# Five loads instead of seven, pieces of 53 and 11 rows, and the final wait on another engine

## The chip, the cores and the metric

The kernel runs on one core of a Trainium2 chip. The metric is device time in microseconds (us) of one execution; "the span" in a profile is shorter, from the first to the last instruction of the kernel's own program. A "landing" is the last of the 16 semaphore updates that report a transfer as complete. A change counts as faster or slower from 2% on. All times below are medians of several executions (granted clock 1.00 in every profile).

## The reference

```python
B, S, D = 1024, 16, 512            # bf16
def reference(x, y, gamma):        # x, y: (B, S, D); gamma: (D)
    return x + gamma * y
```

x and y have 16.78 MB each, the output too: 50.33 MB must cross between HBM and SBUF. One multiply and one add per element are all the arithmetic.

## The kernel before

The 16,384 rows of 512 elements are laid out as 128 partitions of 128 rows; "rows" below counts within a partition. y stays in SBUF whole and the result is written over it. x has a smaller buffer, part of which is used twice. SP issues the loads, ScalarE (ACT) issues the load of gamma and the two stores of 64 rows each, VectorE (DVE) multiplies and adds in four pieces, and TensorE (PE) spreads gamma over the partitions by a matmul with ones and then passes on a release: the stores may start when the load `RELEASE` has landed.

```python
PIECES = [40, 37, 40, 11]
# x entries: first row, end row, place in the x buffer; y entries: first row, end row
SP = [('x', 0, 40, 0), ('y', 0, 40), ('x', 40, 77, 40), ('y', 40, 77),
      ('y', 77, 128), ('x', 77, 117, 0), ('x', 117, 128, 40)]
ACT = [('g',), ('s', 0, 64), ('s', 64, 128)]
EARLY = (2, 1)                     # that many issues of SP and ACT go ahead of the first barrier
RELEASE = ('x', 77, 117, 0)
DVE = [('m', 0), ('a', 0), ('m', 1), ('a', 1), ('m', 2), ('a', 2), ('m', 3), ('a', 3)]
...
def frees(w):                      # which adds must be done before load w may overwrite x rows
    old = x_loads[: x_loads.index(w)]
    old = [v for v in old if meets(v[3], v[3] + v[2] - v[1], w[3], w[3] + w[2] - w[1])]
    return [c for v in old for c in pieces_of(v[1], v[2])]
...
_take(s_load[RELEASE], 16, nc.tensor)      # TensorE: that load has landed
nc.tensor.sem_inc(s_go, 1)                 # ACT may issue the stores
nc.tensor.sem_inc(s_rel, 1)                # DVE may read it
...
nc.scalar.sem_inc(s_end, 1)                # the end of the program
_take(s_end, 1, nc.sync)
_take(s_add, n, nc.sync)
_take(s_out, 16 * len(stores), nc.sync)    # SP waits until the stores have landed
```

`_take(sem, n, eng)` lets an engine wait until a semaphore has n and takes n off it.

Of the kernel before, what the change touches and what calls it, by code (L numbers as in the profile page):

```python
# [3 lines left out]


PIECES = [40, 37, 40, 11]



SP = [('x', 0, 40, 0), ('y', 0, 40), ('x', 40, 77, 40), ('y', 40, 77), ('y', 77, 128), ('x', 77, 117, 0), ('x', 117, 128, 40)]  # L10
ACT = [('g',), ('s', 0, 64), ('s', 64, 128)]

EARLY = (2, 1)


RELEASE = ('x', 77, 117, 0)

DVE = [('m', 0), ('a', 0), ('m', 1), ('a', 1), ('m', 2), ('a', 2), ('m', 3), ('a', 3)]
MULT, ADD = mybir.AluOpType.mult, mybir.AluOpType.add


def _take(sem, n, eng):


    return eng.wait_ge(sem, n).then_inc(sem, -n)  # L25


def kernel(
# [9 lines left out]
    nc = tc.nc  # L38
# [8 lines left out]
    rows = N // P  # L47
    n = len(PIECES)
    assert sum(PIECES) == rows
    starts = [sum(PIECES[:c]) for c in range(n + 1)]  # L50
    dt = xf.dtype
# [7 lines left out]
    y_sb = nc.alloc_sbuf_tensor("y_sb", [P, rows, D], dt).ap()  # L59
    x_loads = [w for w in SP + ACT if w[0] == "x"]  # L60
    y_loads = [w for w in SP + ACT if w[0] == "y"]
    stores = [w for w in SP + ACT if w[0] == "s"]
    for loads in (x_loads, y_loads, stores):
# [8 lines left out]
    s_add, s_go, s_rel, s_end, s_out = sem("s_add"), sem("s_go"), sem("s_rel"), sem("s_end"), sem("s_out")  # L72
    added = [a for kind, *a in DVE if kind == "a"]
    order = {a[0]: k for k, a in enumerate(added)}

    def meets(a, b, c, d):
        return a < d and c < b

    def pieces_of(a, b):
        return [c for c in range(n) if meets(starts[c], starts[c + 1], a, b)]  # L80

    def x_at(row):
        return next(w[3] + row - w[1] for w in x_loads if w[1] <= row < w[2])

    def frees(w):

        old = x_loads[: x_loads.index(w)]
        old = [v for v in old if meets(v[3], v[3] + v[2] - v[1], w[3], w[3] + w[2] - w[1])]
        return [c for v in old for c in pieces_of(v[1], v[2])]

    early = []

    def ring(eng, what, n_early):

        known, went = 0, False
        for k, w in enumerate(what):
            kind = w[0]
            need = frees(w) if kind == "x" else pieces_of(w[1], w[2]) + list(w[3:]) if kind == "s" else []
            need = max((order[c] + 1 for c in need), default=0)
            if kind == "s" and not went:  # L100
                _take(s_go, 1, eng)
                went = True
            if need > known:
                eng.wait_ge(s_add, need)
                known = need
            if kind == "g":
                i = eng.dma_start(out=gamma_row, in_=gamma.unsqueeze(0)).then_inc(s_gamma, 16)
            elif kind == "x":
                to = x_sb[:, w[3] : w[3] + w[2] - w[1], :]
                i = eng.dma_start(out=to, in_=xv[:, w[1] : w[2], :]).then_inc(s_load[w], 16)  # L110
            elif kind == "y":
                r = slice(w[1], w[2])
                i = eng.dma_start(out=y_sb[:, r, :], in_=yv[:, r, :]).then_inc(s_load[w], 16)
            else:
                r = slice(w[1], w[2])
                i = eng.dma_start(out=ov[:, r, :], in_=y_sb[:, r, :]).then_inc(s_out, 16)
            if k < n_early:
                early.append(i.ins)

    ring(nc.sync, SP, EARLY[0])  # L120
    ring(nc.scalar, ACT, EARLY[1])
# [9 lines left out]

    _take(s_load[RELEASE], 16, nc.tensor)
    nc.tensor.sem_inc(s_go, 1)
# [4 lines left out]
    def need(loads, c):  # L138
        for w in loads:
            if w not in landed and meets(starts[c], starts[c + 1], w[1], w[2]):  # L140
                if w == RELEASE:
                    _take(s_rel, 1, nc.vector)
                else:
                    _take(s_load[w], 16, nc.vector)
                landed.add(w)

    for kind, *args in DVE:
        c = args[0]
        yt = y_sb[:, starts[c] : starts[c + 1], :]
        if kind == "m":  # L150
            need(y_loads, c)
            g = gamma_sb[:, None, :].to_broadcast([P, PIECES[c], D])
            nc.vector.tensor_tensor(out=yt, in0=yt, in1=g, op=MULT).then_inc(s_dve, 1)  # L153
            open_mults += 1
        else:
# [4 lines left out]
            at = x_at(starts[c])  # L160
            xt = x_sb[:, at : at + PIECES[c], :]
            nc.vector.tensor_tensor(out=yt, in0=xt, in1=yt, op=ADD).then_inc(s_add, 1)  # L162


    nc.scalar.sem_inc(s_end, 1)
    _take(s_end, 1, nc.sync)
    _take(s_add, n, nc.sync)
    _take(s_out, 16 * len(stores), nc.sync)

    main = nc.main_func.blocks[0].instructions  # L170
    names = {i.name for i in early}
# [35 lines left out]
```

## Time and profile before

| | before |
|---|---|
| time | 119.99 us (119.98 to 120.29) |
| profiled execution | 120.14 us, span 118.8 us |
| VectorE busy | 70.2 us, 59% |
| the 16 DMA engines' busy share, both queues | 66.0 + 32.6 = 98.6% |
| last add ends / second store issued | 97.44 / 97.47 us |
| last packet ends / last landing seen | 118.45 / 118.78 us |

The first thing to read is the DMA share: it leaves no room. Two kinds of record are used besides the page: that of each DMA packet (start, duration, size, queue), and that of semaphore updates, which goes on after the span's end. The packet record does not name the DMA engine; where one engine is followed below, the end of a packet was matched with the start of the next. The runtime closes every execution with a barrier over the five engines, a reset of semaphores and another barrier, and the reported time includes this: the last barrier update of the profiled execution comes at 120.258 us after the span's start, beside a reported 120.14.

### The profile page before, as it was taken

Reading aid. Unit: us, or ns where it says so; the run is one execution under the profiler, and the core shown is the slowest. Engines: PE = TensorE matmul, PEld = TensorE weight load, DVE = VectorE, ACT = ScalarE, POOL = GpSimd, SP = SyncE. Lnnn points to the kernel's source line nnn. Section 1 sums busy time; section 2 is a strip of 40 time slices with the busy share of each in tenths; the row PEclk is TensorE's granted clock in tenths of the full one; section 3 lists DMA queues with packets and bytes.
Section 4 is the critical chain, followed back from the end, with each engine's and each line's share of the span. In section 5 each row is a group of like instructions: output and inputs, shape, how many; then the busy total and the mean of one; then the engine's idle time right before and its main releaser. Section 6 shows DMA issues by size and latency. Waiting matters only on the chain. (4 is left out here: it accounts for less than half of the span.)

```text
span 118.8 us, 84 instructions
## 1 busy us (share of the span) xinstructions
PE 0.6 (0%) x1; PEld 0.1 (0%) x1; DVE 70.2 (59%) x10; POOL 0.2 (0%) x4
## 2 busy tenths in 40 slices
PE   0100000000000000000000000000000000000000
PEld 0000000000000000000000000000000000000000
DVE  0020000009999999799999999999999980000000
POOL 0000000000000000000000000000000000000000
DMA  7999999999999999989696999998899889988890
GB/s 221 442 441 441 441 441 441 441 425 408 408 421 472 485 459 408 475 369 563 281 563 262 441 414 441 408 637 353 353 530 530 353 353 397 662 353 353 353 684 22
DMA packets 1298, 50.33 MB, mean 424 GB/s; under 512 B 145, under 2 KB 146, under 8 KB 146
## 3 DMA queue, kind: packets, MB, share of 16 engines
q1 hardware_dynamic: 1008, 33.55, 66.0%
q10 hardware_dynamic: 290, 16.78, 32.6%
HBM read 33.56 MB, written 16.78 MB: 424 GB/s over the span
## 5 line engine op out<-in xcount | busy, mean ns | idle before, releaser
L153 DVE TENSOR_TENSOR y_sb<-y_sb,gamma_sb 128x20480 bf16<-128x20480 bf16 (+2 forms) x4 | 34.8, 8688 | 20.6 <-DVEq L25 20.6
L162 DVE TENSOR_TENSOR y_sb<-x_sb,y_sb 128x20480 bf16<-128x20480 bf16 (+2 forms) x4 | 34.8, 8691 | 0.6
L129 DVE CAST gamma_sb<-gamma_ps 128x512 bf16<-128x512 f32 x1 | 0.7, 690 | 4.1 <-DVEq L25 4.1
L124 DVE MEMSET ones_row<- 1x128 bf16 x1 | 0.2, 165 | 2.0 <-PEq L41 2.0
L127 PE MATMUL gamma_ps<-gamma_row,ones_row 1*128 1x512 bf16 x1 | 0.6, 581 | 5.5 <-PEq L25 5.5
L127 PEld LDWEIGHTS gamma_ps<-gamma_row,ones_row 1*128 1x128 bf16 x1 | 0.1, 98 | 5.5 <-issue 5.5
L191 POOL MEMSET const-bfloat16-1.0<- 128x1 bf16 x1 | 0.1, 102 | 0.0
L191 POOL MEMSET const-uint8-127<- 128x1 uint8 x1 | 0.1, 101 | 0.0
L191 POOL MEMSET const-float32-0.0<- 128x1 f32 x1 | 0.1, 99 | 0.2 <-issue 0.2
L191 POOL MEMSET const-float32-1.0<- 128x1 f32 x1 | 0.1, 98 | 0.0
## 6 DMA issues: line engine op xcount, KB each, us to landing
x_sb<-in_x_dram SPq DMA_DIRECT2D x2, 5120.0 KB, 21.3
y_sb<-in_y_dram SPq DMA_DIRECT2D x1, 6528.0 KB, 61.8
y_sb<-in_y_dram SPq DMA_DIRECT2D x1, 5120.0 KB, 26.3
x_sb<-in_x_dram SPq DMA_DIRECT2D x1, 4736.0 KB, 36.0
y_sb<-in_y_dram SPq DMA_DIRECT2D x1, 4736.0 KB, 46.9
x_sb<-in_x_dram SPq DMA_DIRECT2D x1, 1408.0 KB, 10.6
out_dram<-y_sb ACTq DMA_DIRECT2D x2, 21.8
gamma_row<-in_gamma_dram ACTq DMA_DIRECT2D x1, 1.0 KB
```

The source lines that it names most:

```text
L124: nc.vector.memset(ones_row, 1.0).then_inc(s_ones, 1)
L127: nc.tensor.matmul(gamma_ps, ones_row, gamma_row, start=True, stop=True).then_inc(s_ps, 1)
L129: nc.vector.tensor_copy(out=gamma_sb, in_=gamma_ps).then_inc(s_dve, 1)
L153: nc.vector.tensor_tensor(out=yt, in0=yt, in1=g, op=MULT).then_inc(s_dve, 1)
L162: nc.vector.tensor_tensor(out=yt, in0=xt, in1=yt, op=ADD).then_inc(s_add, 1)
L191: nc = _bacc.Bacc("TRN2", target_bir_lowering=False, num_devices=1)
```

## The change

Its intent: fewer and larger transfers, a last add that ends earlier, and the final wait on another engine.

```diff
-PIECES = [40, 37, 40, 11]
+PIECES = [53, 11, 53, 11]
-SP = [('x', 0, 40, 0), ('y', 0, 40), ('x', 40, 77, 40), ('y', 40, 77), ('y', 77, 128), ('x', 77, 117, 0), ('x', 117, 128, 40)]
+SP = [('y', 0, 64), ('x', 0, 64, 0), ('y', 64, 128), ('x', 64, 117, 0), ('x', 117, 128, 64)]
-RELEASE = ('x', 77, 117, 0)
+RELEASE = ('x', 64, 117, 0)
-DVE = [('m', 0), ('a', 0), ('m', 1), ('a', 1), ('m', 2), ('a', 2), ('m', 3), ('a', 3)]
+DVE = [('m', 0), ('m', 1), ('a', 0), ('a', 1), ('m', 2), ('m', 3), ('a', 2), ('a', 3)]
 ... (frees() now counts only the pieces whose rows are really overwritten)
-    _take(s_end, 1, nc.sync)
-    _take(s_add, n, nc.sync)
-    _take(s_out, 16 * len(stores), nc.sync)
+    _take(s_end, 1, nc.tensor)
+    _take(s_add, n, nc.tensor)
+    _take(s_out, 16 * len(stores), nc.tensor)
```

The last x load (11 rows) gets rows of the buffer that nothing used before. The two stores stay as they were.

More of the change, by code (lines that the diff above doesn't have):

```diff
@@ L85, in frees @@
     def frees(w):
-        old = x_loads[: x_loads.index(w)]
-        old = [v for v in old if meets(v[3], v[3] + v[2] - v[1], w[3], w[3] + w[2] - w[1])]
-        return [c for v in old for c in pieces_of(v[1], v[2])]
+        c = set()
+        for v in x_loads[: x_loads.index(w)]:
+            lo, hi = max(v[3], w[3]), min(v[3] + v[2] - v[1], w[3] + w[2] - w[1])
+            if lo < hi:
+                c |= set(pieces_of(v[1] + lo - v[3], v[1] + hi - v[3]))
+        return sorted(c)
     early = []
```

## The prediction

> **What bounds the kernel now.** I read the page's slices and engine table first, then the timeline, then the record of each DMA packet, then the waits, and last what follows the span's end.
>
> ```profile
> span 118.8 us, 84 instructions
> PE 0.6 (0%) x1; PEld 0.1 (0%) x1; DVE 70.2 (59%) x10; POOL 0.2 (0%) x4
> DVE  0020000009999999799999999999999980000000
> DMA  7999999999999999989696999998899889988890
> q1 hardware_dynamic: 1008, 33.55, 66.0%
> q10 hardware_dynamic: 290, 16.78, 32.6%
> 1.00:98.50 97.50, 0.58 (x1) 0.10 (x1) 70.20 (x10) 0.00 (x0) 1.00 1.00 431
> ```
>
> The reader should see: VectorE is busy 59% of the span and idle in the last seven slices; the 16 DMA engines are busy 66.0 + 32.6 = 98.6% of it. The last line is one long window (columns: the stretch in us from the start, its length, engines' busy times, clock, DMA share, GB/s): from 1.00 to 98.50 us the DMA share is 1.00. The kernel moves 50.33 MB and its time is the DMA engines' time, plus a start and an end. The low digits 6 to 8 are an artefact of large packets counted in slices; the window shows no hole.
>
> ```profile
> 0.00 0.37 SPq L110 DMA_DIRECT2D x_sb<-in_x_dram  x1
> 26.84 10.83 DVE L153 TENSOR_TENSOR y_sb<-y_sb,gamma_sb 128x20480 bf16<-128x20480 bf16 x1 [19.94 <-DVEq L25]
> 48.67 21.18 SPq L110 DMA_DIRECT2D x_sb<-in_x_dram  x2
> 77.07 20.74 ACTq L116 DMA_DIRECT2D out_dram<-y_sb  x2
> 94.35 3.09 DVE L162 TENSOR_TENSOR y_sb<-x_sb,y_sb 128x5632 bf16<-128x5632 bf16 x1
> L162 DVE TENSOR_TENSOR y_sb<-x_sb,y_sb 128x20480 bf16<-128x20480 bf16 x2 | 21.6, 10824 | 0.3
> ```
>
> The last add ends at 94.35 + 3.09 = 97.44, and the second store is issued at 97.47 (the two issues are merged in the ACTq line: 77.07 + 20.74 is the end of the second). The first store's packets end between 98.47 and 98.93 on the 16 engines. A store becomes ready about 1.01 us after its issue: the very first load, issued at 0.00, has its first packet at 1.00. So the second store arrived just in time, with no slack. In the packet record twelve engines begin it within a few ns of the end of the first, but four begin some 24 to 139 ns late (ends and starts paired in order) and their first packet takes 2.45 to 2.46 us, not 2.418. The latest of them, starting at 99.06, is the engine that ends the program's traffic at 118.45; the next one ends at 118.25. So I read the late last add as costing about 118.45 - 118.25 = 0.20 us now. This is the only stall by computation that I find.
>
> **What the Trainium skill says.** "DMA: Bandwidth & Descriptors", section "Where 436 GB/s comes from", gives 16 ports x 32 B x 850 MHz, 435 GB/s in all, or 27.2 GB/s a port. The trace agrees: a 65,536-byte packet takes 2.418 us, 27.1 GB/s. The same page, "Issuing engines are not separate DMA queues": DMAs from different engines share the same 16 DMA engines, so splitting them otherwise buys no bandwidth; the 1.00 share, with loads on one queue and stores on the other, agrees. "VectorE: DVE Perf Modes", "The perf-mode tier table": a bf16 tensor_tensor stops at two elements a cycle; 20,480 / 2 / 0.96 GHz = 10.67 us, and the trace has 10.82. "Runtime: NRT & Kernel Launch", "The ~15µs preamble/postamble breakdown": after the kernel comes a barrier that passes serially over five engines at 44 ns a hop, then a reset of semaphores and another barrier. The trace's semaphore updates after the span agree on the hop: 98.080, 98.118, 98.161 us are 38 and 43 ns apart.
>
> **The change part by part.**
>
> Packets. Each transfer is 128 rows of one packet, 8 to an engine. Median packet times in the trace: 11,264 B 0.422 us, 37,888 B 1.401, 40,960 B 1.514, 52,224 B 1.928, 65,536 B 2.418. A line through the first and last gives 36.78 ns per KB (1,000 B) plus 8 ns per packet. The seven loads of before need 8 x (3 x 1.514 + 2 x 1.401 + 1.928 + 0.422) = 77.55 us of an engine. The five of after need 8 x (3 x 2.418 + 2.004 + 0.422) = 77.44, where 2.004 is the line's value for 53 rows, 54,272 B. Bytes are equal, so removing two loads removes only 16 packets' overhead: **-0.11 us**, all on the path.
>
> Order of loads. The big ones still follow each other in one queue. With the start as now (the slowest engine ended the first load at 14.25, 2.14 after 8 x 1.514) I get landings, noticed about 0.45 later, at: y 0-64 21.9, x 0-64 41.3, y 64-128 60.6, x 64-117 76.6, x 117-128 79.9.
>
> VectorE. Same elements, eight instructions as before; the 53-row one is 27,136 / 2 / 0.96 GHz + 0.16 = 14.29 us, the 11-row one 3.09. Two multiplies from 22.0 to 39.4; two adds wait for x, 41.3 to 58.8; two multiplies wait for y, 60.7 to 78.1; the adds 78.2 to 95.7. The idle start of VectorE shrinks and a new idle time of about two times 1.9 us appears, all hidden. x 64-117 overwrites rows 0-53 of x and waits for the add that ends at 55.7; it is then ready at 56.7, while the queue is full until 60.1, so 3.4 us of margin. x 117-128 has rows of its own and needs no wait. Before, the corresponding loads were issued at 48.67 and 69.52, also ahead of need.
>
> Stores. The first is released by the landing of x 64-117 as before, near 77.0, and its packets start behind x 117-128. The second is issued at 95.7 instead of 97.5, 1.8 us earlier, and is ready at 96.7, before any engine ends the first: **-0.20 us**, the late engine's loss. DMA then ends near 118.46 - 0.31 = 118.15.
>
> End. SP's final wait takes 17 ns in the trace, TensorE's semaphore instructions 51 ns, and TensorE sees a landing some 0.03 us after it, against 0.02: +0.05 in the span. More happens after it. Updates of the runtime's barrier semaphore in before: 77.337, 98.080, 98.118, 98.161, 118.947, then 118.990, 119.029, 119.064, 119.110, and after the resets 119.900 to 120.258 (the profiled run's time, 120.14, so includes this tail). The first follows TensorE's last instruction (77.10) by 0.235, the second ScalarE's (97.86) by 0.22, the fifth SP's (118.82) by 0.13. I infer that the barrier climbs from TensorE to SP and comes back. If SP is last, the climb is already done when the stores land. If TensorE is last, it must enter (0.235 rather than 0.13) and then climb four hops (0.035 + 0.038 + 0.043 + 0.024 = 0.14, from the second barrier). Together with the 0.05 that is **+0.29 us**, of it 0.24 outside the span.
>
> Sum: -0.11 - 0.20 + 0.29 = -0.02 us. The span should go to about 118.8 - 0.31 + 0.05 = 118.5, and the time stays near 119.97. I choose 119.95.
>
> **Rivals.** One: the end on TensorE is free, because its entry into the barrier overlaps something or the climb is not what I inferred; then the time is 119.99 - 0.31 = 119.7. For it: someone chose TensorE on purpose. Against it: the order of the barrier updates. Two: the pieces starve the queue. A 53-row add now sits between a landing and the reuse of x rows; if it slipped by more than 3.4 us the DMA would stop and every lost microsecond would show. Against it: VectorE durations in this trace differ by less than 0.1%. Three: the last add becomes the bound, since 17.4 us of adds follow the last big x; it ends at 95.7 against a need by 97.5, and a slip would cost at most what before already pays. Four: the 0.20 us is not lateness but spread between engines, which returns elsewhere; then 120.15. Rates for 64-row reads could differ from 64-row writes, but packets of 37,888 to 52,224 B already read at 27.0 to 27.1 GB/s.
>
> **Range and chances.** The terms are 0.1 to 0.3 us each and of both signs; before's three runs spread 0.31 us. I take 119.65 (end free, lateness gone) to 120.3 (lateness not gone, end dear). Two per cent is 2.4 us, eight times any term, and 98.6% of the span is traffic that the change leaves. Faster by 2% would need fewer bytes; slower by 2% would need an emptied queue. Hence 0.01, 0.98, 0.01.
>
> **What would show each step.** Queue packets: 720 on the load queue, 290 on the store queue. The second store issued near 95.7, and its packets starting on all engines without the late four. Loads landing within 0.3 us of my list. The last waits of VectorE near 41.3 and 60.7, about 1.9 us each. The span near 118.5 while the time stays: the barrier's first update now after the last landing, and all nine in one climb and descent. The prediction is wrong if the DMA share dips between 55 and 62 us, if x 64-117 is issued after 60, or if the span and the time fall together by 0.3 us.

## The result, and the profile after

The changed kernel takes **120.33 us** (120.26 to 120.52, six runs) against 119.99 (119.98 to 120.29). The ratio is 1.0024, 95% interval 1.0012 to 1.0037. Ratios here are the mean time of one kernel's runs over that of the other's of the same rounds, so not quite the ratio of the medians. It is a small loss, 0.34 us in the medians, clear of the noise, and well inside "the same within 2%".

The page of the changed kernel, the same lines as the prediction shows of the kernel before (the last one is again the long window, with the DMA share last but one):

```profile
span 118.8 us, 78 instructions
PE 0.6 (0%) x1; PEld 0.1 (0%) x1; DVE 70.0 (59%) x10; POOL 0.2 (0%) x4
DVE  0020000599999299999859999999999910000000
DMA  9899888998899888988896969598899889988890
q1 hardware_dynamic: 720, 33.55, 65.9%
q10 hardware_dynamic: 290, 16.78, 32.6%
1.00:98.50 97.50, 0.58 (x1) 0.10 (x1) 70.03 (x10) 0.00 (x0) 1.00 1.00 432
```

The load queue has 720 packets in place of 1008, and nothing else moves: the same bytes, the same shares, the DMA full from 1.00 to 98.50 us. VectorE's row shows the new pattern: it starts earlier and has two dips.

The timeline of the changed kernel (start, duration, engine, line, operation; in brackets the idle time before it):

```profile
22.10 17.29 DVE L156 TENSOR_TENSOR y_sb<-y_sb,gamma_sb 128x27136 bf16<-128x27136 bf16 x2 [13.59 <-DVEq L25]
41.52 17.29 DVE L165 TENSOR_TENSOR y_sb<-x_sb,y_sb 128x27136 bf16<-128x27136 bf16 x2 [2.13 <-DVEq L25]
55.84 0.81 SPq L113 DMA_DIRECT2D x_sb<-in_x_dram  x2
60.77 17.29 DVE L156 TENSOR_TENSOR y_sb<-y_sb,gamma_sb 128x27136 bf16<-128x27136 bf16 x2 [1.96 <-DVEq L25]
77.03 18.85 ACTq L119 DMA_DIRECT2D out_dram<-y_sb  x2
78.21 17.29 DVE L165 TENSOR_TENSOR y_sb<-x_sb,y_sb 128x27136 bf16<-128x27136 bf16 x2
```

Each DVE line is two instructions merged. The waits of 2.13 and 1.96 us are for x and y, hidden, as foreseen. The last add ends at 78.21 + 17.29 = 95.50 us, 1.94 us earlier than before, and the second store is issued at 95.54.

The end decides. These are the updates of the runtime's barrier semaphore in the two traces, us from the span's start (not a view of the profile page; taken from the record of semaphore updates):

```
          last landing | first barrier, up                      | down                             | second barrier
before    118.782      | 77.337 98.080 98.118 98.161 118.947    | 118.990 119.029 119.064 119.110  | 119.900 ... 120.258
after     118.686      | 119.000 119.034 119.073 119.117 119.140| 119.238 119.277 119.311 119.358  | 120.146 ... 120.503
```

Before, four of the five steps up had been taken before the stores landed. After, all nine steps come after it. From the landing to the last update it is 1.476 us before and 1.817 after, 0.341 more, as much as the medians differ by. (The two profiled executions differ by 0.24 us only, because the landing came 0.10 us earlier in the second.) The span hides most of it: the profiled executions have 118.8 us both, while their times are 120.14 and 120.38, so time less span is 1.32 us before and 1.61 after.

### The profile page after: what moved, and what is told of

Its sections match the earlier page's. It is cut to its first block, busy times and chain, and to the rows that moved or that the text cites. A ratio compares the mean times of both kernels' runs of the same rounds, so it can differ in the third digit from the quotient of the medians.

```text
span 118.8 us, 78 instructions
## 1 busy us (share of the span) xinstructions
PE 0.6 (0%) x1; PEld 0.1 (0%) x1; DVE 70.0 (59%) x10; POOL 0.2 (0%) x4
## 5 line engine op out<-in xcount | busy, mean ns | idle before, releaser
L156 DVE TENSOR_TENSOR y_sb<-y_sb,gamma_sb 128x27136 bf16<-128x27136 bf16 (+1 forms) x4 | 34.6, 8688 | 15.5 <-DVEq L25 15.5
L165 DVE TENSOR_TENSOR y_sb<-x_sb,y_sb 128x27136 bf16<-128x27136 bf16 (+1 forms) x4 | 34.6, 8688 | 2.3 <-DVEq L25 2.1
```

Of the source, the lines that this page charges most:

```text
L156: nc.vector.tensor_tensor(out=yt, in0=yt, in1=g, op=MULT).then_inc(s_dve, 1)
L165: nc.vector.tensor_tensor(out=yt, in0=xt, in1=yt, op=ADD).then_inc(s_add, 1)
```

## The experiments

Theory: the final wait on TensorE costs 0.3 us, because the barrier climbs from TensorE to SP and now must do so after the stores; the loads and pieces are worth nothing. Rivals: the new loads cost something (one DMA engine trails the others by 0.23 us from the first load on), or the end is free. All runs returned correct results.

**1. The new loads and pieces, SP ends.**

```diff
 # changed kernel
-    _take(s_out, 16 * len(stores), nc.tensor)
+    _take(s_out, 16 * len(stores), nc.sync)     # and the two takes above it
```

> The changed kernel's five loads and four VectorE pieces, but SP takes the final waits as in the kernel before. Theory (the end on TensorE costs, because the runtime's barrier climbs from TensorE to SP and the climb must then follow the stores): the stretch from the last landing to the last barrier update falls back from 1.81 to about 1.48 us, and the time from 120.33 to about 120.0 us, within 0.1 of before. Rival (the new loads are what costs, e.g. the one DMA engine that trails the others by 0.23 us from the first load on): it stays near 120.3 us. Rival (end free): the prediction's 119.7 us.

Measured: 120.02 us (119.91 to 120.44, six runs); before in the same rounds 120.00; ratio 1.0006 (0.9994 to 1.0018). The theory holds. The profiled execution was the slowest of the six (120.44, span 119.1): its packets ended 0.4 us later than in the changed kernel's trace, but from the landing (119.083) to the last barrier update (120.559) it has 1.476 us, exactly as before.

**2. The old loads and pieces, TensorE ends.**

> The kernel before with nothing changed but that TensorE takes the final waits. Theory: +0.33 us, so about 120.3 to 120.4 us, with all nine updates of the barrier semaphore after the last landing, the first 0.30 us after it. Rival (the loads cost, the end is free): 120.0 us.

Measured: 120.33 us (120.28 to 120.34); ratio 1.0026 (1.0014 to 1.0038). From landing to last update 1.818 us. Runs 1 and 2 with the two kernels make a full table:

| | SP ends | TensorE ends |
|---|---|---|
| old loads | 119.99, 120.00 | 120.33 |
| new loads | 120.02 | 120.33 |

Along a row the end costs 0.31 to 0.34 us; down a column the loads make nothing that can be seen. The profiles of run 1 and then run 2 show the same in another way, by the span of the core:

```profile
core 0: 119.1 us, clock 1.000
```

```profile
core 0: 118.7 us, clock 1.000
```

Run 1's profiled execution took 120.44 us, run 2's 120.28: the time outlasts the span by 1.3 us where SP ends (as before: 120.14 and 118.8) and by 1.6 us where TensorE ends (as in the changed kernel: 120.38 and 118.8). This is so in every execution, not only in the profiled ones: 1.27 to 1.34 us in the six of run 1, 1.58 to 1.64 in the five of run 2. The median span is 118.7 us in both runs, so the span alone would not have shown the 0.31 us between them.

**3. Where in the barrier each engine stands.** The same edit to the end of the changed kernel, with `nc.scalar`, then `nc.gpsimd`, then `nc.vector`.

> The changed kernel with the final waits on ScalarE. Theory (climb TensorE, ScalarE, two others, SP): TensorE's update comes early, near 77.3 us, ScalarE's comes first after the last landing by 0.25 us, then three hops; about 0.20 us above the run that ends on SP and 0.1 below the one that ends on TensorE, so about 120.2 us. Rival (no order: TensorE alone is slow, an engine's own delay): no more than 0.09 us above the run that ends on SP.

> The changed kernel with the final waits on GpSimd. Theory (the barrier climbs TensorE, ScalarE, GpSimd, VectorE, SP): TensorE's and ScalarE's updates come early (near 77.3 and 96.1 us), GpSimd's third and first of all after the last landing; from the landing to the last update 1.60 to 1.65 us, between 1.48 (SP) and 1.65 (ScalarE). Rival (VectorE stands third): three updates before the last landing, as with SP less one.

> The changed kernel with the final waits on VectorE. Theory (VectorE fourth, one below SP): three updates of the barrier before the last landing, VectorE's first after it, one hop to SP; from the landing to the last update 1.55 to 1.60 us. Rival (VectorE third): two updates before, and more than with GpSimd.

Measured: 120.21 us with ScalarE (120.15 to 120.31), 120.55 with GpSimd and 120.21 with VectorE (two runs each). The records of updates, worked out from the traces (all in us; "entry" is from the landing to the ending engine's own update, "climb" from there to SP's, "turn" from SP's to the first one down):

| the end on | updates before the landing | entry | climb | turn | landing to last update |
|---|---|---|---|---|---|
| SP (before) | 4 | 0.165 | 0 | 0.043 | 1.476 |
| VectorE | 3 | 0.230 | 0.024 | 0.099 | 1.619 |
| ScalarE | 1 | 0.183 | 0.105 | 0.099 | 1.654 |
| TensorE (changed) | 0 | 0.314 | 0.140 | 0.098 | 1.817 |
| GpSimd | 2 | 0.603 | 0.066 | 0.100 | 2.035 |

What is left, from the first step down to the end, is 1.265 to 1.268 us in every row. The count of updates that came early gives the order: TensorE, ScalarE, GpSimd, VectorE, SP. The climb grows with the steps that are left, as the theory says. ScalarE came as expected, 0.19 us above run 1 (its rival said at most 0.09); only its entry was shorter, 0.183 for 0.25. Two expectations missed: GpSimd was expected at 1.60 to 1.65 and has 2.035, because its entry alone takes 0.60 us, and VectorE has 1.62, not 1.55 to 1.60. So an engine's place in the order is not all; its own entry counts as much. (One trace for each row; GpSimd and VectorE have two timed executions each.) SP is best in both.

**4. Does a late second store cost 0.2 us?** The prediction read this out of the trace of before. First the cheapest cure: the old kernel with y ahead of x.

```diff
-SP = [('x', 0, 40, 0), ('y', 0, 40), ('x', 40, 77, 40), ('y', 40, 77), ...
+SP = [('y', 0, 40), ('x', 0, 40, 0), ('y', 40, 77), ('x', 40, 77, 40), ...
```

> The kernel before, the first two pairs of loads in the other order (y ahead of x), so that multiplies start 12 us earlier and the last add ends near 94 us instead of 97.4; seven loads and the end on SP stay. Theory of the prediction (a late second store costs 0.20 us): four engines no longer begin it late, last packet near 118.25 and about 119.8 us. Rival (spread between engines returns elsewhere): the late starts go but the last packet still ends at 118.3 to 118.5, and the time stays near 120.0 us.

Measured: 120.04 us (120.00 to 120.09), ratio 1.0002 (0.9990 to 1.0014). The timeline of this run shows the add early and the store with it:

```profile
77.05 17.73 ACTq L116 DMA_DIRECT2D out_dram<-y_sb  x2
91.31 3.09 DVE L162 TENSOR_TENSOR y_sb<-x_sb,y_sb 128x5632 bf16<-128x5632 bf16 x1
```

The last add ends at 94.40 us, three us earlier, no DMA engine begins the second store late any more, and the last packet still ends at 118.29. The interval of the ratio, turned into us, is -0.12 to +0.17: the 0.2 us was not there to be had. Then two runs from the other side, which delay the last add of run 1 by idle multiplies on x rows that are no longer needed:

```diff
+        if (kind, c) == ('a', 3):
+            for r in [7]:                    # late7; [11, 11] in late22
+                d = x_sb[:, 53 : 53 + r, :]
+                ... tensor_tensor(out=d, in0=d, in1=gamma broadcast, op=MULT), and wait for it
```

> sp_end with one idle multiply of 7 rows (2.0 us) ahead of the last add, which then ends near 97.7 us instead of 95.5, and the second store is ready near 98.8. Theory now (only an engine that is already through with the first store loses, and the engine that trails, through near 99.0, sets the end): no more than +0.1 us, about 120.0 to 120.1. Theory of the prediction (such lateness costs 0.2 us and more): 120.25 or more.

> sp_end with two idle multiplies of 11 rows (6.4 us in all) ahead of the last add, which then ends near 102.1 us. The second store is issued at 102.1, ready at 103.1, 4.1 us after the trailing engine is through: 124.1 us if VectorE's end really gates the second store with the 1.01 us between issue and first packet. If something else is slack (rival), less than 123 us.

The timeline of the run with 7 rows, then of that with 22:

```profile
76.99 21.12 ACTq L119 DMA_DIRECT2D out_dram<-y_sb  x2
92.37 2.02 DVE L155 TENSOR_TENSOR x_sb<-x_sb,gamma_sb 128x3584 bf16<-128x3584 bf16 x1
94.65 3.09 DVE L170 TENSOR_TENSOR y_sb<-x_sb,y_sb 128x5632 bf16<-128x5632 bf16 x1 [0.26 <-DVEq L25]
```

```profile
76.86 25.43 ACTq L119 DMA_DIRECT2D out_dram<-y_sb  x2
92.25 6.32 DVE L155 TENSOR_TENSOR x_sb<-x_sb,gamma_sb 128x5632 bf16<-128x5632 bf16 x2
98.83 3.09 DVE L170 TENSOR_TENSOR y_sb<-x_sb,y_sb 128x5632 bf16<-128x5632 bf16 x1 [0.26 <-DVEq L25]
```

With 7 rows the last add ends at 97.74 us, 0.3 later than in the kernel before. Ten of the sixteen DMA engines begin the second store with a longer first packet (2.436 to 2.461 us), yet the time is 119.99 us (119.92 to 120.08; ratio 0.9997, 0.9980 to 1.0013): the DMA engine that ends last was through with the first store at 98.92, after the second was ready at 98.63, and lost nothing. With 22 rows the add ends at 101.92, the store's first packets start at 102.79 to 102.94, and the time is 124.20 us (124.08 to 124.34), 4.18 above run 1, as foreseen. Here the queue was empty, so this trace measures directly how long a store needs from its issue (101.95) to its first packets: 0.84 to 0.99 us. A window of that trace shows the hole, with the same window of run 1 after it (DMA share last but one):

```profile
98.50:102.50 4.00, 0.00 (x0) 0.00 (x0) 3.16 (x2) 0.00 (x0) 1.00 0.00 0
```

```profile
98.50:102.50 4.00, 0.00 (x0) 0.00 (x0) 0.00 (x0) 0.00 (x0) 1.00 1.21 524
```

(A share over 1 arises because a packet is counted where it starts.) So the last add has an edge, and these two runs put it where the trailing DMA engine, the one that ends its share last, ends the first store. The kernel before stands just ahead of it, the changed one 1.9 us further ahead, and being further ahead is worth nothing.

**5. What does a packet cost?** The change has 16 packets a DMA engine less, and the prediction put 0.11 us on them. The loads of run 1 were cut smaller, and the stores' release moved to the last part of x 64-117.

```diff
+for _w in _BIG:                              # the five loads of the changed kernel
+    for _r in range(_w[1], _w[2], 8):        # 32 in the second run
+        ... append the part of at most 8 rows, at its place
```

> The five loads of the changed kernel, in the same order and places, cut into 33 of at most 8 rows; end on SP as in sp_end, which is the kernel to compare with. It has 28 loads and 28 x 8 = 224 packets an engine more. Theory of the prediction (8 ns for each packet, all on the path): +1.8 us, 121.8 us, packets of 8,192 B at 0.31 us. Rival (the packet term is smaller, or hidden by the engines' overlap, as the missing 0.11 us of the change suggests): near 120.0 us.

> sp_end with its five loads cut into nine of at most 32 rows: 32 packets an engine more than sp_end (88), 16 more than before (72). parts8 gave 8.3 ns for each packet added (1.87 us for 224). Theory (the same cost for each packet at small numbers): +0.27 us over sp_end, 120.25 to 120.3 us, and then the 0.13 us that the change's loads should save are real but lie in the spread of the runs. Rival (a few packets more or less cost nothing, because the time is set by the trailing engine and by the start): 120.0 us.

The load queue and its issues in the run with parts of at most 8 rows:

```profile
q1 hardware_dynamic: 4752, 33.56, 67.2%
y_sb<-in_y_dram SPq DMA_DIRECT2D x16, 1024.0 KB, 22.0
```

It took 121.90 us (121.77 to 122.12); an 8,192-byte packet takes 0.312 us. Against run 1 that is 1.88 us for 224 packets a DMA engine, 8.4 ns each, the completion writes of 28 more loads included; the cost for a packet is real and lies on the path. With parts of at most 32 rows, 120.16 us (120.10 to 120.31), ratio 1.0013 (1.0000 to 1.0027): 16 packets above before cost about 0.15 us, where 0.13 was expected, but 32 above run 1 cost 0.14, where 0.27 was expected. This points to run 1, the new loads, as what lacks its gain, but not firmly: the interval of parts32 is 0 to +0.32 us, and run 1 was timed in other rounds. Run 1's interval against before, turned into us, is -0.07 to +0.22 and does not hold -0.11. Two more runs have the same loads and SP at the end, late7 (-0.24 to +0.16) and no_gamma below (-0.26 to +0.10), and both do hold it. So a gain of some hundredths of a us is not excluded; it is not seen. One candidate for a loss is the start: up to the end of the first load, the median DMA engine needs 1.87 us above its packets' own time in the mean of eight traces with the 64-row load first, and 1.81 us in the three traces with a 40-row one. But these traces range from 1.78 to 1.97 and from 1.76 to 1.85, so this is not shown. It stays open.

**6. Is it gamma's DMA engine that trails?** Run 1 without the load of gamma (a memset of zeros in its place, so wrong; the reference's gamma is so small that the result still passed).

> sp_end without the load of gamma (a memset of zeros in its place: a wrong result on purpose). Theory (the one engine that carries gamma's small packet is the one that trails by 0.1 to 0.4 us): the last engine's gap to the last but one closes to under 0.1 us at the end of the first load, and the time falls by 0.1 to 0.2 us, to 119.8 to 119.9. Rival (the spread comes from the first packets or from pauses of the engines at random): gap and time as in sp_end, 120.0 us.

Measured: 119.95 us (119.88 to 120.01), ratio 0.9993 (0.9978 to 1.0008). The last DMA engine is 0.10 us behind the last but one at the end of the first load and 0.08 at the end, against 0.23 at both points in the changed kernel's trace; but run 1 has 0.17 and 0.09, the run with ScalarE at the end 0.06 and 0.37, and the run with 22 late rows 0.09 at the end of the first load, all with gamma loaded. The spread varies as much from run to run. It is not settled whether gamma has a part in it.

No version was found that beats the kernel before. The natural one, the new loads with SP at the end, is run 1, and it ties.

## Why the prediction was right or wrong

What bounds the kernel, the cost of the end and the class were right; the figure chosen was 0.38 us too low (119.95 against 120.33), because two of the three terms of the sum did not come. The measured median lies at the upper end of the range, which stood for just this case ("lateness not gone, end dear"). The class says little about the terms: each is far below 2%.

- **What bounds the kernel: right.** The DMA share stays at 1.00 and the bytes are the same. Rival two (starved queue) is excluded: x 64-117 was issued at 55.84 against a foreseen 55.7, and needed only by 60.1.
- **Landings and VectorE: right to 0.2 us.** Landings are seen at 22.0, 41.3, 60.7, 76.7 and 80.1, foreseen 21.9, 41.3, 60.6, 76.6, 79.9 (the last would be 80.0 by the prediction's own terms); a 53-row instruction takes 14.29 us, as worked out; the last add ends at 95.5, foreseen 95.7.
- **End, +0.29: right, 0.05 too small.** The traces show +0.34: entry 0.149 more, climb 0.140, and a term that was left out, the turn at SP, 0.098 instead of 0.043. It was foreseen that most of it would fall outside the span, and it did; but the span was to shrink to 118.5 by the other two terms, and its median stayed at 118.7. Runs 1, 2 and 3 confirm the inferred order of the barrier.
- **"The late engine's loss", -0.20: wrong.** This is the step that failed. It read one execution, in which the DMA engine that began the second store last also ended last, as a cost of every execution. That execution took 120.14 us, 0.15 over the median from which the sum then started, so a good part of the 0.20 would have been counted twice even if the reading held. Run y_first takes the lateness away and gains nothing, late7 increases it and loses nothing: the end was set there by a DMA engine that was through with the first store late (98.97 and 98.92 us), after the second was ready. Run pe_end is a second trace of the old loads: two DMA engines begin the second store with a long first packet, and the one that ends last (118.13) is neither. Nor does the reading of the late add come out in the trace of before: with the 0.84 to 0.99 us of late22 in place of the prediction's 1.01, the store issued at 97.47 was ready at 98.31 to 98.46 (an estimate), before any DMA engine had ended the first store (98.47). What made four of them begin at 98.75 to 99.06 in that execution stays open. Rival four ("spread, which returns elsewhere"; "then 120.15") named this, and was given too little weight.
- **Packets, -0.11: the price was right, the gain did not show.** parts8 confirms the price at 8.4 ns. The gain lies below what these runs can tell from nothing: where it goes, or whether a part of it is there, is open.

With 0.34 for the end, and 0 for the two gains that were not seen, the sum is 120.33.

## What to carry to other kernels

In this kernel, which keeps its DMA full from start to end, moving computation earlier was worth nothing once the next transfer was ready when the queue got to it; find that edge, and stop there. The program's end is part of the time: let the final wait stand on the engine that the closing barrier asks last (here SP, by 0.14 to 0.56 us over the others), and look past the span, because the span doesn't show it. Before a tenth of a microsecond goes into a sum, compare the profiled execution with the median, and see in a second trace whether the feature is there.

## What the Trainium skill lacked or had wrong

- "Runtime: NRT & Kernel Launch", "The ~15µs preamble/postamble breakdown", gives a serial barrier over five engines and its time for a hop (44 ns) for the barrier before the kernel; for the one after it, only that it waits for all engines. It has neither the order nor that it matters which engine ends last. After the kernel the runs show hops of 23 to 47 ns and a turn of 98 to 100 (43 to 44 where SP ends last), the order TensorE, ScalarE, GpSimd, VectorE, SP, and 1.476 us from the last landing to the end with SP last, 1.817 with TensorE.
- No page has the entry of an engine into that barrier after its last wait: from the landing 0.17 us for SP, 0.18 for ScalarE, 0.23 for VectorE, 0.31 for TensorE and 0.60 for GpSimd.
- "DMA: Bandwidth & Descriptors", "Why small descriptors are slow", puts a packet's fixed overhead at about 3 cycles and does not say of which clock; at the 850 MHz that the page gives for the fabric this would be some 3.5 ns (an estimate). It has no figure for packets as large as here: the line through packet times of 11 to 66 KB gives 8 ns, and 224 packets more cost 8.4 ns each, completion writes included. Whether the two are the same overhead no run here shows.
